# Layer 2's first product in seven block products instead of eight, with streamed weights and a list schedule for the second half

## The chip, the cores and the metric

The program runs on one core of a Trainium2 chip. The metric is device time in microseconds (us), the median of three runs. The engines are TensorE (PE, matrix products), VectorE (DVE), ScalarE (ACT), GpSimd (POOL) and SyncE (SP, which here issues all DMAs).

## The reference, cut to what matters

Attention with a decaying state gives x, 3072 tokens of 512 features; two feed-forward layers follow.

```python
x = attn_out.transpose(0, 2, 1, 3).reshape(3072, 512)
h = x @ moe_w_in               # layer 1: 512 -> 2048
x = np.maximum(0.01 * h, h) @ moe_w_out      # 2048 -> 512
h = x @ moe2_w_in              # layer 2: 512 -> 2048
g = np.where(h > 0.0, h, np.exp(np.minimum(h, 0.0)) - 1.0)
out = g @ moe2_w_out           # 2048 -> 512
```

The weights come as 64-bit floats, and the kernel turns them into 32-bit ones by operations on their bits.

## The kernel before

Tokens are cut into six blocks of 512 (`j`, `NB` = 6), the 2048 inner features into sixteen tiles of 128 (`m`, `MF` = 16), the 512 features into four chunks. Every matrix operand is held as a high and a low part (`hi`, `lo`, type fp32r), and each product of two such operands is three matmuls: high by high, high by low, low by high. A step is one pair of block and tile: `gemm1` makes the tile h of 128 by 512 in one PSUM bank with 12 matmuls (four chunks by three), an activation follows, `split_g` makes its two parts (`ghi` on ACT, `glo` on DVE), and `gemm2` adds the tile's share to the four banks `y` of the block with 12 matmuls. `ph` is 0 in layer 1 and 1 in layer 2.

The order of the work is that of the code, engine by engine; the program adds waits where data or a buffer demands them. Three stretches matter. From about 69 to 153 us the first steps of layer 1 are emitted by `scheduled`: tasks with an engine, a cost and dependencies are placed by a greedy rule, always the task that can begin first, the more urgent one among equals. From about 175 to 525 us steps of layer 1 alternate with attention for later blocks, and `pre` converts layer 2's weights: 32 pieces of 128 by 512, each loaded, converted on ACT and DVE, split on ACT and POOL, and written to DRAM (`wscr`). After that come the last block of layer 1 (block 5, from `NA` on) and layer 2, about 620 to 1142 us. There all weights of layer 2 lie in SBUF, loaded once by `load_w2` into the places of layer 1's, and each step runs `gemm1` for tile s, the activation (`elu_act`, four ACT instructions; `elu_dve`, four DVE instructions one step later), and `gemm2` for tile s-3:

```python
nta = elu_act(h)
if last is not None:
    split(s - 1, last, nc.vector)
d = drain(s - 3, stage_o)
last = elu_dve(h, *nta)
```

`drain` calls `gemm2`, and behind a block's last tile copies the four banks out and stores them: `yscr` in DRAM for layer 1, `out` for layer 2. Layer 2 loads a block of `yscr` back (`load_x`) and splits it into `xhi` and `xlo` (`split_x`).

Of the kernel before, what the change touches and what calls it, by code (L numbers as in the profile page):

```python
# [32 lines left out]
P = 128  # L33
# [11 lines left out]
V0 = 4  # L45

# [8 lines left out]
def body(ctx: ExitStack, tc: tile.TileContext, kkv, w1, w2, tabs, out):  # L55
# [10 lines left out]
    wscr = [dp.tile([P, 4, BLK], F32, name=f"wscr{m}") for m in range(MF)]  # L66
# [9 lines left out]
    nload = nload2 = 0  # L76
# [20 lines left out]

    def load_w2():

        nonlocal nload2  # L100
        m = nload2
        for a in range(2) if m < V0 else (0,):
            n = 1 if m < V0 else 2
            t = place(m, a, n, F32R, "w")
            nc.sync.dma_start(out=t.bitcast(F32), in_=wscr[m][:, 2 * a : 2 * (a + n), :].rearrange("p a c -> p (a c)"))
            for i in range(n):
                wt[1, m, a + i] = t[:, i * W : (i + 1) * W]
        nload2 += 1

# [111 lines left out]
    through = []  # L221

    def pre_load():
        k = npre
        if k < 2 * MF:
            t = cv.tile([P, W], U32, tag="f", name="raw2")
            m, a = divmod(k, 2)
            nc.sync.dma_start(out=t, in_=w2[m][:, a * BLK : (a + 1) * BLK].bitcast(U32))
            through.append(t)
# [3 lines left out]
    def pre(more):  # L233
# [5 lines left out]
        m, a = divmod(npre, 2)  # L239
        npre += 1  # L240
        if more:
            pre_load()
        both = cv.tile([P, W], U16, tag="e", name="e2")
        e, sg = both[:, :BLK], both[:, BLK:]
        f = cv.tile([P, BLK], F32, tag="s", name="f2", bufs=1)
# [3 lines left out]
        top(t, f)  # L249
        low(t, f)  # L250
        sign(e, sg)
        power(e, f)
        r = t.bitcast(F32R)
        nc.scalar.copy(r[:, :BLK], f)
        nc.gpsimd.tensor_tensor(r[:, BLK:], f, r[:, :BLK].bitcast(F32), ALU.subtract)
        nc.sync.dma_start(out=wscr[m][:, 2 * a : 2 * a + 2, :], in_=r.rearrange("p (a c) -> p a c", a=2).bitcast(F32))
# [97 lines left out]
    with ExitStack() as actx:  # L354
# [330 lines left out]
        for n, (s, upto) in enumerate(plan[NL:], NL):  # L685
# [17 lines left out]
            if vi > 3:  # L703

                if m == 2 and npre < 2 * MF:
                    pre_load()
                if 2 < m < MF - 1:
                    pre(m < MF - 2)
# [4 lines left out]
    with ExitStack() as ectx:  # L713
        ep = ectx.enter_context(tc.tile_pool(name="ep", bufs=2))
        eps = ectx.enter_context(tc.tile_pool(name="eps", bufs=3, space=PSUM))
        xs = {}

        def stage_o():
            for _ in range(4):
                yield ep.tile([P, BLK], F32, tag="osb", name="osb", bufs=4)  # L720

        def load_x(j, i):
            t = ep.tile([P, 2, BLK], F32, tag="xs", name="xs")
            nc.sync.dma_start(out=t, in_=yscr[j][:, 2 * i : 2 * i + 2, :])
            xs[j, i] = t

        def split_x(j, k):
            b, t = j % 2, xs[j, k // 2][:, k % 2, :]
            nc.scalar.copy(xhi[b][:, k, :], t)
            nc.vector.tensor_tensor(xlo[b][:, k, :], t, xhi[b][:, k, :].bitcast(F32), ALU.subtract)  # L730

        def elu_act(h):
            n = ep.tile([P, BLK], F32, tag="n", name="n")
            t = ep.tile([P, BLK], F32, tag="t", name="t")
            a = ep.tile([P, BLK], F32, tag="a", name="a2")
            nc.scalar.activation(n, h, AF.Relu, scale=-1.0)  # L736
            nc.scalar.activation(t, n, AF.Tanh, scale=-0.5)  # L737
            nc.scalar.activation(a, t, AF.Copy, bias=-0.5, scale=0.5)
            nc.scalar.activation(n, n, AF.Exp, scale=-1.0)  # L739
            return n, t, a  # L740

        def elu_dve(h, n, t, a):
            gf = gp.tile([P, BLK], F32, tag="gf", name="gf2", bufs=2)
            nc.vector.scalar_tensor_tensor(out=a, in0=n, scalar=1.0, in1=a, op0=ALU.add, op1=ALU.mult)  # L744
            nc.vector.scalar_tensor_tensor(out=t, in0=n, scalar=1.0, in1=t, op0=ALU.add, op1=ALU.mult)  # L745
            nc.vector.scalar_tensor_tensor(out=t, in0=a, scalar=2.0, in1=t, op0=ALU.add, op1=ALU.mult)  # L746
            nc.vector.scalar_tensor_tensor(out=gf, in0=h, scalar=0.0, in1=t, op0=ALU.max, op1=ALU.add)  # L747
            return gf

        def split(s, gf, eng):  # L750
            if s % 4 == 3:
                split_g(s, gf, eng, ep, 1)
            else:
                split_g(s, gf, eng, gp, 3)

        comes = {(0, len(VISITS[0]) - 1): 0, **{(1, j): j + 1 for j in range(NB - 1)}}
        last = None
        for s in range(NA, 2 * NS):
            ph, j, m, (_, _, m0, m1, vi) = steps[s]
            if s % 4 == 0:  # L760
                h = ps.tile([P, BLK], F32, tag="h", name="h")
            else:
                h = eps.tile([P, BLK], F32, tag="h2", name="h2")
            gemm1(ph, m, j % 2, h)
            if ph == 0:
                gf = leaky(h)
                d = drain(s - (2 if s < NA + 4 else 3), stage_o)
                split(s, gf, nc.vector)
            else:
                nta = elu_act(h)  # L770
# [76 lines left out]
```

## Time and profile before

| | before |
|---|---|
| median of three runs | 1148.68 us (1148.34 to 1148.70) |
| profiled execution, first to last instruction (span) | 1146.8 us |
| PE busy | 1132.1 us, 99% of the span |
| DVE busy | 650.8 us, 57% |
| ACT busy | 542.7 us, 47% |
| bytes moved by DMA | 117.10 MB |

No time of its own is given for the profiled execution beside its span; the median of the runs is 1.9 us more than the span, which is what lies around the first and the last instruction. Busy time counts an engine's own instructions and not its waits. PE's instructions overlap, so a busy PE need not be one at its peak; what tells is the time from one matmul to the next. In the rows, L268 is `gemm1`, L291 `gemm2`, L562 the second product in `scheduled`, L736 to L747 the activation of layer 2, L274 and L275 the split of g, L325 the copies out of PSUM.

### The profile page before, as it was taken

Reading aid. Unit: us, or ns where it says so; the run is one execution under the profiler, and the core shown is the slowest. Engines: PE = TensorE matmul, PEld = TensorE weight load, DVE = VectorE, ACT = ScalarE, POOL = GpSimd, SP = SyncE. Lnnn points to the kernel's source line nnn. Section 1 sums busy time; section 2 is a strip of 40 time slices with the busy share of each in tenths; the row PEclk is TensorE's granted clock in tenths of the full one; section 3 lists DMA queues with packets and bytes.
Section 4 is the critical chain, followed back from the end, with each engine's and each line's share of the span. In section 5 each row is a group of like instructions: output and inputs, shape, how many; then the busy total and the mean of one; then the engine's idle time right before and its main releaser. Section 6 shows DMA issues by size and latency. Waiting matters only on the chain.

```text
span 1146.8 us, 14900 instructions
## 1 busy us (share of the span) xinstructions
PE 1132.1 (99%) x6024; PEld 928.2 (81%) x6024; DVE 650.8 (57%) x1047; ACT 542.7 (47%) x899; POOL 92.7 (8%) x77
## 2 busy tenths in 40 slices
PE   8899999999999999999999999999999999999998
PEld 6678888788888888888888888888888888888886
DVE  5999913246544663641213766765765666666655
ACT  2576621234444443432324655555555655655553
POOL 4000001102222221210000000000000000000000
PEclk9999999999999999999999999999999999999999
DMA  9912313345544544522556200100100100000100
GB/s 377 418 41 89 131 37 111 111 135 201 200 161 167 190 178 139 193 93 68 189 185 219 92 19 1 55 19 1 55 19 1 55 19 1 37 1 1 38 1 37
DMA packets 29302, 117.10 MB, mean 102 GB/s; under 512 B 3249, under 2 KB 3249, under 8 KB 23217
## 3 DMA queue, kind: packets, MB, share of 16 engines
q1 hardware_dynamic: 29232, 116.15, 27.4%
q8 instruction: 47, 0.77, 0.3%
q14 instruction: 23, 0.18, 0.1%
HBM read 84.68 MB, written 31.46 MB: 101 GB/s over the span
## 4 chain that ended last, share of the span: by engine, by line
PE 94%; DVE 4%; DMA 1%; ACT 0%; issue 0%; SPq 0%; ACTq 0%
PE h L268 44%; PE y L291 41%; PE y L562 4%; PE sc L398 2%; PE o L416 2%; DMA kv<-in_kkv 1%; PE o L424 1%; PE o L420 1%; DVE f L127 1%; DVE pt L404 0%; DVE f L134 0%; DVE xlo L441 0%; DVE e L131 0%; DVE w L181 0%; DVE s L116 0%; DVE f L123 0%
## 5 line engine op out<-in xcount | busy, mean ns | idle before, releaser
L268 PE MATMUL h<-xhi,w 128*128 128x512 f32 x1536 | 505.7, 391 | 1.1 <-ACT gf L350 1.1
L268 PEld LDWEIGHTS h<-xhi,w 128*128 128x128 f32 x1536 | 288.2, 188 | 63.1 <-ACT gf L350 1.5
L275 DVE TENSOR_TENSOR glo<-gf,ghi 128x512 fp32r<-128x512 f32 x171 | 119.3, 698 | 370.5 <-ACT ghi L274 370.5
L268 PE MATMUL h<-xlo,w 128*128 128x512 f32 x768 | 299.0, 389 | 0.0
L291 PE MATMUL y<-w,ghi 128*128 128x512 f32 x768 | 236.4, 389 | 0.0
L291 PE MATMUL y<-ghi,w 128*128 128x512 f32 x616 | 204.3, 393 | 0.0
L291 PEld LDWEIGHTS y<-w,ghi 128*128 128x128 f32 x768 | 144.1, 188 | 29.9
L268 PEld LDWEIGHTS h<-xlo,w 128*128 128x128 f32 x768 | 144.2, 188 | 29.5
L736 ACT ACTIVATE n<-h 128x512 f32<-128x512 f32 x96 | 57.5, 599 | 224.3 <-PE h L268 224.3
L291 PE MATMUL y<-w,glo 128*128 128x512 f32 x384 | 149.4, 389 | 0.0
L350 ACT ACTIVATE gf<-h 128x512 f32<-128x512 f32 x96 | 57.2, 596 | 186.7 <-PE h L268 186.3
L291 PEld LDWEIGHTS y<-ghi,w 128*128 128x128 f32 x616 | 115.6, 188 | 26.4 <-issue 2.4
L291 PE MATMUL y<-glo,w 128*128 128x512 f32 x308 | 119.9, 389 | 0.0
L274 ACT CAST ghi<-gf 128x512 fp32r<-128x512 f32 x171 | 104.7, 612 | 5.3 <-DVE gf L747 3.4
L291 PEld LDWEIGHTS y<-w,glo 128*128 128x128 f32 x384 | 72.2, 188 | 15.0
L744 DVE SCALAR_TENSOR_TENSOR a<-n,a 128x512 f32<-128x512 f32 x96 | 65.7, 685 | 5.9 <-ACT n L739 5.9
L746 DVE SCALAR_TENSOR_TENSOR t<-a,t 128x512 f32<-128x512 f32 x96 | 66.4, 692 | 3.3
L747 DVE SCALAR_TENSOR_TENSOR gf<-h,t 128x512 f32<-128x512 f32 x96 | 66.4, 691 | 3.3
L291 PEld LDWEIGHTS y<-glo,w 128*128 128x128 f32 x308 | 57.8, 188 | 11.6
L120 ACT ACTIVATE e<-e,ebias 128x512 int16<-128x512 uint16 (+1 forms) x52 | 42.7, 821 | 50.7 <-DVE e L117 50.5
L745 DVE SCALAR_TENSOR_TENSOR t<-n,t 128x512 f32<-128x512 f32 x96 | 65.9, 686 | 0.0
L737 ACT ACTIVATE t<-n 128x512 f32<-128x512 f32 x96 | 60.7, 632 | 3.1
(59 smaller groups left out, 924.8 us busy)
## 6 DMA issues: line engine op xcount, KB each, us to landing
kv<-in_kkv SPq DMA_DIRECT2D x23, 1024.0 KB, 6.5
raw<-in_w SPq DMA_DIRECT2D x40, 512.0 KB, 3.8
wscr<-raw SPq DMA_DIRECT2D x32, 512.0 KB, 2.6
raw<-in_w SPq DMA_DIRECT2D x12, 1024.0 KB, 12.3
w<-wscr SPq DMA_DIRECT2D x12, 1024.0 KB, 4.8
xs<-yscr SPq DMA_DIRECT2D x12, 512.0 KB, 3.6
out<-osb SPq DMA_DIRECT2D x24, 256.0 KB, 3.8
yscr<-ysb SPq DMA_DIRECT2D x16, 256.0 KB, 2.7
```

The lines of the kernel that those rows point to most:

```text
L268: nc.tensor.matmul(h, a, x, start=(n == 0), stop=(n == 3 * KD - 1))
L274: nc.scalar.copy(ghi, gf)
L275: eng.tensor_tensor(glo, gf, ghi.bitcast(F32), ALU.subtract)
L291: nc.tensor.matmul(acc[d], lhsT, rhs, start=(first and n == 0), stop=(last and n == 2))
L350: nc.scalar.activation(gf, h, AF.Prelu, alpha=0.01)
L562: nc.tensor.matmul(acc[i][:, d % 2], lhsT, rhs, start=(m == m0 and n == 0), stop=(m == m1 - 1 and n == 2))
L736: nc.scalar.activation(n, h, AF.Relu, scale=-1.0)
L737: nc.scalar.activation(t, n, AF.Tanh, scale=-0.5)
L744: nc.vector.scalar_tensor_tensor(out=a, in0=n, scalar=1.0, in1=a, op0=ALU.add, op1=ALU.mult)
L745: nc.vector.scalar_tensor_tensor(out=t, in0=n, scalar=1.0, in1=t, op0=ALU.add, op1=ALU.mult)
L746: nc.vector.scalar_tensor_tensor(out=t, in0=a, scalar=2.0, in1=t, op0=ALU.add, op1=ALU.mult)
L747: nc.vector.scalar_tensor_tensor(out=gf, in0=h, scalar=0.0, in1=t, op0=ALU.max, op1=ALU.add)
```

## The change

Layer 2's first product is done for two token blocks at once (`q` = 0, 1, 2 stands for blocks 2q and 2q+1) and for two tiles at once (`i` and `i + 8`), so that one group is a product of 2 by 2 blocks: X11, X12, X21, X22 (token block by half of the 512 features) times W11, W12, W21, W22 (half of the features by tile). Strassen's scheme in Winograd's form needs seven products of 6 matmuls where the plain way has eight:

```
S1 = X21+X22   S2 = S1-X11   S3 = X11-X21   S4 = X12-S2
T1 = W12-W11   T2 = W22-T1   T3 = W22-W12   T4 = T2-W21
bank px:  X11 W11 | + S2 T2 -> copied for h12 | + S3 T3 -> h22 | - X22 T4 -> h21
h11 = X11 W11 (copied from px) + X12 W21 (bank pv)
h22 += S1 T1 (bank pq);   h12 += S1 T1 + S4 W22 (bank pq, added to)
```

(h11 and h12 are the two tiles of block 2q, h21 and h22 those of block 2q+1.) The T's are made once, in `pre`, in the stretch of attention: eight of the 32 conversions get five more instructions on DVE, two on ACT and one on POOL, and with their eight neighbours they write seven operands per group to `w1scr`. The S's are made on DVE once for each pair of blocks: four instructions of 1024 elements a partition, and the split of seven X operands is seven such instructions on ACT and seven on DVE.

From the second step of block 5 on, everything is tasks of one list: PE's order is fixed (two or three pieces of second products behind each product, a piece being the three matmuls of one bank), ACT, DVE and SP are ordered by the greedy rule. The h tiles are copied from PSUM to SBUF and have the activation in place there; up to 32 of them and their successors live in the places that layer 1's weights leave. The second products run through the blocks in order; the first of layer 2 stands behind five groups, so behind ten tiles of block 0. Weights are no longer kept: each product loads its operand of 256 KB (`w1r`, six buffers), each second product's tile its 512 KB (four buffers), again for each block: 264 loads in place of 20.

```diff
-    def load_w2():
...
-            nc.sync.dma_start(out=t.bitcast(F32), in_=wscr[m][:, 2 * a : 2 * (a + n), :].rearrange("p a c -> p (a c)"))
...
+        i, n = m - HM, QB
+        fi = kept.pop(i)
...
+        sub(tw[:, 1, 1], g[:, n:], g[:, :n], ALU.subtract)
+        sub(tw[:, 0, 1], g[:, :n], gi[:, :n], ALU.subtract)
+        sub(g[:, :n], g[:, n:], tw[:, 0, 1], ALU.subtract)
+        sub(gi[:, n:], gi[:, n:], g[:, :n], ALU.subtract)
+        nc.scalar.copy(tt[:, :, 0], tw[:, :, 1])
+        sub(tt[:, :, 1], tw[:, :, 1], tw[:, :, 0], ALU.subtract)
+        nc.sync.dma_start(out=w1scr[i][:, 3:5, :], in_=t.bitcast(F32).rearrange("p (b c) -> p b c", b=2))
+        halves_of(g, pw)
+        nc.scalar.copy(fi[:, :n], gi[:, n:])
+        nc.gpsimd.tensor_tensor(fi[:, n:], gi[:, n:], gi[:, :n], ALU.subtract)
...
+        stock["w1"] = [lazy(lambda k=k: ep.tile([P, BLK], F32R, name=f"w1r{k}")) for k in range(6)]
+        stock["g"] = [lazy(lambda k=k: ep.tile([P, BLK], F32, name=f"g{k}")) for k in range(4)]
...
+        ORDER = ("11", "12", "s2", "s1", "s3", "22", "s4")
+        PAUSE = (2, 2, 2, 2, 3, 2, 3)
...
+            task(("mk", q, "s1"), "V", 1.25, [("ld", q, "21"), ("ld", q, "22")],
+                 lambda rt=rt: mix(rt("s"), rt("21"), rt("22"), add), use=[T("21"), T("22")], take=("t", T("s")))
...
+                    task(("xh", q, n), "A", 1.05, [seen, ("mk", q, n) if n != "22" else ("ld", q, "22")],
+                         lambda q=q, n=n, src=src: x_hi(q, n, src), use=[key], take=("x", X(n)))
...
+        def product(q, i, k):
+            n = ORDER[k]
+            hi, lo = at(("x", q, n))
+            w = at(("w1", q, i, k))
+            to = bank[("px", "pv", "px", "pq", "px", "px", "pq")[k]]
+            first = k in (0, 1, 3)
+            z = 0
+            for c in range(2):
+                wh, wl = w[:, c * P : (c + 1) * P], w[:, QB + c * P : QB + (c + 1) * P]
+                for a, x in ((wh, hi[:, c]), (wh, lo[:, c]), (wl, hi[:, c])):
+                    nc.tensor.matmul(to, a, x, start=(first and z == 0), stop=(z == 5), skip_group_check=True)
+                    z += 1
...
+            def snap(b, k):
+                task(("c", *hk[b]), "A", 0.62, [P_(k)], lambda: nc.scalar.copy(at(("h", *hk[b])), bank["px"]), take=("g", ("h", *hk[b])))
+
+            def plus(b, name, deps):
+                t = ("h", *hk[b])
+                task(("s", *hk[b]), "V", 0.7, [("c", *hk[b])] + deps, lambda: tt(at(t), at(t), bank[name], add), use=[t])
...
+            return [prod(0, [prior("c", "21")]), prod(1, [prior("s", "11")]), prod(2, [("c", *hk["11"])]),
+                    prod(3, [prior("s", "12"), freed]), prod(4, [("c", *hk["12"])]), prod(5, [("c", *hk["22"])]), prod(6, [("s", *hk["22"])])]
...
+        filler(48)
+        before = None
+        for q in range(SB):
+            for i in range(HM):
+                for x, n in zip(group_tasks(q, i, before), PAUSE if q < SB - 1 or i < HM - 2 else (1, 2, 2, 1, 2, 2, 2)):
+                    put_pe(x)
+                    filler(n)
+                before = q, i
+        filler(10**6)
```

The seven products are numbered k = 0 to 6 in the order of `ORDER`; p0 to p6 below. A product waits for the copy or the addition that frees its bank: the last lines of `group_tasks` name them.

On PE, before, in layer 2 (h2 is the bank of a first product, y the banks of a second one, numbers tell buffers apart), a second product and the next first one stand like this:

```order
L291 MATMUL y1_7187<-w_4907,ghi_7520 128x512 x2
L291 MATMUL y1_7187<-w_4907,glo_7521 128x512
L268 MATMUL h2_7623<-xhi1_100,w_5055 128x512
L268 MATMUL h2_7623<-xlo1_102,w_5055 128x512
L268 MATMUL h2_7623<-xhi1_100,w_5055 128x512 x2
```

On PE, now, in the third group of the second pair of blocks: p4, three pieces of second products (of 3 matmuls each), p5, the next piece. Here xhi0 and xlo0 are places that now hold both parts of one X operand, ws a streamed weight of the second product:

```order
L996 MATMUL px_4535<-xhi0_107,w1r2_4615 128x512 x6
L1083 MATMUL y_4585<-ws_5407,ghi_4663 128x512 x2
L1083 MATMUL y_4585<-ws_5407,glo_4668 128x512
L1083 MATMUL y_4585<-ws_5407,ghi_4663 128x512 x2
L1083 MATMUL y_4585<-ws_5407,glo_4668 128x512
L1083 MATMUL y_4586<-ws_5407,ghi_4663 128x512 x2
L1083 MATMUL y_4586<-ws_5407,glo_4668 128x512
L996 MATMUL px_4535<-xlo0_109,w1r3_4635 128x512 x6
L1083 MATMUL y_4586<-ws_5407,ghi_4663 128x512 x2
```

The 12 matmuls of a first product in a row have become products of 6 between pieces of second products, and p5 adds to the bank px that p4 wrote, behind 9 matmuls.

On ACT, before, in layer 2, a step is the four activation instructions and the cast of the tile before:

```order
L736 ACTIVATE n_7077<-h2_7064 128x512
L737 ACTIVATE t_7078<-n_7077 128x512
L738 ACTIVATE a2_7079<-t_7078 128x512
L739 ACTIVATE n_7077<-n_7077 128x512
L274 CAST ghi_7084<-gf2_7059 128x512
```

On ACT, now, around the copy of px that lies between that p4 and p5 (the first `L1014` row; nt and a2 are the activation's scratch):

```order
L1095 CAST ghi_4620<-ws_5372 128x512
L1046 ACTIVATE nt_4823<-nt_4823 128x512
L1014 COPY g0_4802<-px_4535 128x512
L1050 ACTIVATE a2_4824<-nt_4823 128x512
L1054 ACTIVATE nt_4823<-nt_4823 128x512
L1042 ACTIVATE nt_4883<-ws_5523 128x512
L1046 ACTIVATE nt_4883<-nt_4883 128x512
L1014 COPY g1_4838<-px_4535 128x512
```

The copies stand between the activation instructions of other tiles, whose scratch (two sets) DVE gives back.

On DVE, now, the addition that p6 of the same group waits for is the `L1018` row; ahead of it stand the activation of an earlier tile and a split:

```order
L1066 SCALAR_TENSOR_TENSOR nt_4883<-a2_4884,nt_4883 128x512
L1098 TENSOR_TENSOR glo_4627<-ws_5372,ghi_4620 128x512
L1070 SCALAR_TENSOR_TENSOR ws_5677<-ws_5677,nt_4883 128x512
L1018 TENSOR_TENSOR g0_4802<-g0_4802,pq_4537 128x512
L1058 SCALAR_TENSOR_TENSOR a2_4824<-nt_4823,a2_4824 128x512
```

The addition is new. Before, a bank of a first product was read by ACT's L736 and, last, by DVE's L747, with four banks in turn; now px is read by copies on ACT alone, and pv and pq by additions on DVE.

## Rows read from the trace of the kernel before

**Rows 1.** The page: span, and its first part (busy time, share, instructions).
```profile
span 1146.8 us, 14900 instructions
...
PE 1132.1 (99%) x6024; PEld 928.2 (81%) x6024; DVE 650.8 (57%) x1047; ACT 542.7 (47%) x899; POOL 92.7 (8%) x77
```

**Rows 2.** Windows: stretch, its length, busy time (instructions) by engine, clock, DMA share, GB/s.
```profile
69.00:153.00 84.00, 83.72 (x369) 69.36 (x370) 73.32 (x95) 52.92 (x63) 1.28 (x1) 1.00 0.26 101
175.00:525.00 350.00, 350.00 (x2196) 284.08 (x2195) 167.18 (x312) 134.00 (x224) 72.61 (x56) 1.00 0.43 154
...
620.00:1142.00 522.00, 522.00 (x2305) 432.17 (x2303) 332.45 (x510) 291.74 (x508) 0.00 (x0) 1.00 0.08 28
```

**Rows 3.** The page: the chain that ended last, by engine.
```profile
PE 94%; DVE 4%; DMA 1%; ACT 0%; issue 0%; SPq 0%; ACTq 0%
```

**Rows 4.** The chain by time, last 28 us: start, length, what.
```profile
1123.26 2.72 PE h L268 x12
...
1131.42 10.89 PE y L291 x48
...
1142.34 0.58 ACT osb L325
```

**Rows 5.** Groups with shapes apart, 620 to 1142 us: ACT.
```profile
L737 ACT ACTIVATE t<-n 128x512 f32<-128x512 f32 x95 | 60.1, 632 | 3.0
...
L274 ACT CAST ghi<-gf 128x512 fp32r<-128x512 f32 x96 | 58.1, 605 | 3.4 <-DVE gf L747 3.4
L736 ACT ACTIVATE n<-h 128x512 f32<-128x512 f32 x95 | 56.9, 599 | 220.1 <-PE h L268 220.1
...
L325 ACT COPY osb<-y 128x512 f32<-128x512 f32 x12 | 6.4, 581 | 0.0
```

**Rows 6.** The same view and stretch: DVE.
```profile
L275 DVE TENSOR_TENSOR glo<-gf,ghi 128x512 fp32r<-128x512 f32 x96 | 66.5, 692 | 181.3 <-ACT ghi L274 181.3
L746 DVE SCALAR_TENSOR_TENSOR t<-a,t 128x512 f32<-128x512 f32 x95 | 65.7, 692 | 3.3
```

**Rows 7.** The same view, whole span: 1024 elements wide.
```profile
L181 DVE TENSOR_TENSOR w<-f,w 128x1024 fp32r<-128x1024 f32 x12 | 14.6, 1220 | 0.6 <-ACT w L177 0.6
...
L177 ACT CAST w<-f 128x1024 fp32r<-128x1024 f32 x12 | 12.6, 1051 | 9.1 <-DVE f L134 9.1
```

**Rows 8.** Timeline, 800 to 812 us: start, length, instruction, [idle before it].
```profile
801.97 0.60 ACT L274 CAST ghi<-gf 128x512 fp32r<-128x512 f32 x1
...
802.61 0.69 DVE L275 TENSOR_TENSOR glo<-gf,ghi 128x512 fp32r<-128x512 f32 x1 [2.09 <-ACT ghi L274]
...
804.63 0.39 PE L268 MATMUL h<-xhi,w 128*128 128x512 f32 x1
...
805.06 0.60 ACT L736 ACTIVATE n<-h 128x512 f32<-128x512 f32 x1 [1.52 <-PE h L268]
```

**Rows 9.** DMA issues: KB each, median us from issue to landing.
```profile
xs<-yscr SPq DMA_DIRECT2D x12, 512.0 KB, 3.6
out<-osb SPq DMA_DIRECT2D x24, 256.0 KB, 3.8
yscr<-ysb SPq DMA_DIRECT2D x16, 256.0 KB, 2.7
```

**Rows 10.** The same timeline: four stores issued by SP.
```profile
803.93 1.94 SPq L326 DMA_DIRECT2D out<-osb  x4
```

**Rows 11.** The page: GB/s moved in each of the 40 slices.
```profile
GB/s 377 418 41 89 131 37 111 111 135 201 200 161 167 190 178 139 193 93 68 189 185 219 92 19 1 55 19 1 55 19 1 55 19 1 37 1 1 38 1 37
```

**Rows 12.** Waits of PE, 69 to 153 us: us in total, times, longest.
```profile
PE y L562 <- DVE glo L593: 0.6, 1, 0.6
```

**Rows 13.** Timeline, 346 to 356 us: a step that converts a weight piece.
```profile
351.10 0.66 ACT L113 COPY e<-raw 128x512 int16<-128x512 int16 x1
...
354.66 0.62 ACT L254 CAST raw<-f 128x512 fp32r<-128x512 f32 x1 [1.44 <-DVE f L134]
...
355.39 0.60 ACT L350 ACTIVATE gf<-h 128x512 f32<-128x512 f32 x1
```

More of the change, by code (lines that the diff above doesn't have):

```diff
@@ L231, in body, with halves_of, pre @@
     npre = 0
-    def pre(more):
+    def halves_of(f, r):
+        nc.scalar.copy(r[:, 0], f)
+        nc.gpsimd.tensor_tensor(r[:, 1], f, r[:, 0].bitcast(F32), ALU.subtract)
+    def pre(more, pool):
         nonlocal npre
@@ L713, in body @@
     with ExitStack() as ectx:
[L714 to L725, printed above, removed]
@@ L784, in body @@
-        split(2 * NS - 1, last, nc.vector)
-        drain(2 * NS - 1, stage_o)
+        ep = ectx.enter_context(tc.tile_pool(name="ep", bufs=1))
+        eps = ectx.enter_context(tc.tile_pool(name="eps", bufs=1, space=PSUM))
+        bank = {n: eps.tile([P, BLK], F32, tag=n, name=n) for n in ("px", "pv", "pq")}
+        bank["h"] = ps.tile([P, BLK], F32, tag="h", name="h")
+        drain(NA - 2, stage_f)
+        gemm1(0, 0, (NB - 1) % 2, bank["h"])
+        drain(NA - 1, stage_f)
+        ys = [ps.tile([P, 2, BLK], F32, tag=f"y{i}", name="y") for i in range(2)]
@@ new lines, in body, with task @@
+        ybank = [ys[d // 2][:, d % 2] for d in range(4)]
+        J = NB - 1
+        tasks, uses, uses_of, places, pe = {}, {}, {}, {}, []
+        def task(key, eng, cost, deps, fn, use=(), take=None, lag=0.0):
+            tasks[key] = eng, cost, [d for d in deps if d is not None], fn, take, lag
+            uses_of[key] = list(use) + ([take[1]] if take else [])
+            for u in uses_of[key]:
+                uses.setdefault(u, []).append(key)
+            if eng == "P":
+                pe.append(key)
@@ new lines, in body, with at, lazy, get @@
+        stock = {}
+        turns_into = {}
+        made = {}
+        def at(key):
+            return places[key]()
+        def lazy(make):
+            got = []
+            def get():
+                if not got:
+                    got.append(make())
+                return got[0]
+            return get
+        def part(get, *index):
+            return lambda: get()[index]
+        def slot(m, dtype=F32R):
+            return lazy(lambda: wp.tile([P, 4, BLK], dtype, tag=f"w{m}", name="ws"))
@@ new lines, in old_second, with old_leaky @@
+        def old_second(s, d):
+            m = steps[s][2]
+            w = wt[0, m, 1]
+            ds = slice(d * P, (d + 1) * P)
+            hi, lo = w[:, ds], w[:, BLK + d * P : BLK + (d + 1) * P]
+            ghi, glo = at(("ghi", s)), at(("glo", s))
+            for n, (a, x) in enumerate(((hi, ghi), (hi, glo), (lo, ghi))):
+                nc.tensor.matmul(ybank[d], a, x, start=(m == 0 and n == 0), stop=(m == MF - 1 and n == 2))
+        def old_leaky(s):
+            nc.scalar.activation(at(("gf", s)), bank[old_bank(s)], AF.Prelu, alpha=0.01)
@@ new lines, in body, with old_steps @@
+        last_of = {}
+        def old_steps():
+            before = None
+            for s in range(NA, NS):
+                m = s - NA
+                for k in range(KD):
+                    yield ("g1", s, k), 0.68 if m else 0.0, [("leaky", s - (2 if m < 5 else 1))] if k == 0 and m > 1 else [], \
+                        (lambda s=s, k=k: old_first(s, k) if s > NA else None), [("w", m), ("x5",)]
+                if before is not None:
+                    yield from old_seconds(before)
+                before = s
+            yield from old_seconds(before)
@@ L788, in _tables @@
+        assert len(over) == len(tasks), [x for x in tasks if x not in over][:20]
 def _tables():
```

385 lines of the change are left out of this document (312 added, 73 removed).

## The prediction

> **What bounds the kernel now.** I read the page first: PE is busy for 1132.1 of the 1146.8 us [rows 1], and the chain of work that ended last is 94% PE [rows 3]. Then the windows, because a share of busy time is a mean over stages: in layer 2, 620 to 1142 us, PE is busy in all 522.00 us at a granted clock of 1.00, while DVE works 332.45 us of them (64%) and ACT 291.74 (56%) [rows 2]. The reader is to see that nothing but the number and the pace of the matmuls sets the end there. The pace is in the chain by time: 12 matmuls take 2.72 us in either product [rows 4], 0.2267 us each. So a matmul left out is worth 0.2267 us for as long as PE still never waits, and the whole question is whether it will.
>
> **What is removed.** Layer 2's first product has 6 blocks by 16 tiles by 12 = 1152 matmuls. Now there are 24 groups of 7 products of 6 = 1008. The 144 matmuls that are gone are all of the same shape as those that stay (512 columns), and at 0.2267 us they are 32.6 us. No matmul is added anywhere: the sums T and S are made on other engines, and adding into px and pq is the accumulation that PSUM does for any product. The second products keep their 1152.
>
> **What is added, per group.** A group makes four tiles and takes along 16 pieces of second products, four tiles' worth: 42 + 48 = 90 matmuls, 20.4 us of PE. In that time:
> DVE runs 16 activation instructions and 4 splits at 0.692 us [rows 6], 13.84 us, and 3 additions. No such addition (SBUF plus PSUM) is in this trace; L275, the same size, takes 0.692, and I use that: 2.08 us. The S's and the splits of X are 11 instructions for 8 groups, at 1.22 us [rows 7] 1.7 us per group. Sum 17.6 us, 86% of 20.4.
> ACT runs 16 activation instructions at no more than 0.632, 4 casts at 0.605, 4 copies of px (L736 reads PSUM at the same size in 0.599) and per group one copy out of y at 0.581 [rows 5]; 7 wide casts at 1.051 for 8 groups [rows 7] add 0.9. Sum 16.4 us, 80%.
> So both stay below PE, but DVE with 2.8 us to spare per group in place of 36%. There is a precedent in the same trace: in the stretch from 69 to 153 us, which the same kind of list orders, DVE is busy 73.32 of 84 us (87%), and PE 83.72 [rows 2]; its only wait there is 0.6 us, once [rows 12]. This is the row on which I lean most.
>
> **The waits on the way.** Which product can be held up is read from the order. p5 is the tightest: it adds to px behind three pieces, 2.04 us, in which ACT must copy px. A copy takes 0.60; the hand from PE to ACT takes 0.04 us (the matmul at 804.63 ends at 805.02, ACT starts at 805.06), and from ACT to DVE as much (802.57, 802.61) [rows 8]. If a wide cast of 1.05 has just begun, the copy still ends 0.04 + 1.05 + 0.60 = 1.69 us after p4, plus a hand back of some 0.04. It fits. p6 has 4.76 us for that copy and one addition of 0.69; the other products have 4.08 us or more. The h tiles have a lead: the shortest is that of the last tile of an even block, made by p6 of a pair's last group and used 15 pieces of 0.68 and six products of 1.36 later, 18 us, for a chain of one addition, four ACT and four DVE instructions, a cast and a split, 7.3 us. Each wait costs nothing while these covers last; uncovered, PE waits for what is missing.
>
> **The loads.** A group needs 7 x 256 KB and 4 x 512 KB, 3.9 MB in 20.4 us, 193 GB/s. Layer 2 moves 28 GB/s now [rows 2], but the second slice of the span shows 418 [rows 11], and from 175 to 525 us PE is busy in every one of the 350 us beside 154 GB/s [rows 2]. A load of 512 KB lands after 3.6 us, one of 256 KB I bound by 2.7 and 3.8 [rows 9]; the six buffers of w1r give each about 17 us, the four of w2 15 us, and 8 us in the last stretch, where only second products are left (three tiles of 2.72). SP issues four stores in 1.94 us [rows 10], 0.49 each, so 13 or so in a group cost it 6.3 us. All of it is hidden; a load that came later than these leads would stop its product and, SP being one queue, the loads behind it.
> The Trainium skill (DMA: Bandwidth & Descriptors, Rules for kernel authors) asks for 1 MiB or more per DMA for the most bandwidth, which speaks against cutting 1 MB weights into 256 KB pieces. The rows differ in what matters here: four stores of 256 KB leave within 1.94 us and land 3.8 us after their issue, so they overlap [rows 9, 10]. The sum above uses the rows and comes to 1117; by the rule, taken so far that each small load pays for itself one after the other, it is rival (c), 1427.
>
> **The stretch of attention.** Eight conversions get five more DVE instructions (at most 0.69 each), two ACT, one POOL. PE has no work in them. In a step that converts, ACT's cast ends at 355.28 and the next leaky starts at 355.39 [rows 13], so what is added moves that leaky back, by 1.2 us (two short copies) to 4.7 (the five DVE instructions in full as well). The next product in the same bank comes three pieces of 2.72 us later, 8.2 us. DVE is busy 167.18 and ACT 134.00 of 350 us there [rows 2]. Cost nothing; if the cover failed, at most 4.7 us eight times, which I hold for very unlikely. The loads of kv are issued two chunks ahead and only move behind a few more stores on SP.
>
> **The beginning and the end.** ACT's order puts two casts of the first X blocks ahead of the leaky of block 5's third step, and their loads now stand on SP behind block 4's four stores (1.94 us). Such a step has 5.44 us for 1.9 us of leaky, cast and split, so a lateness of 2 to 3 us is about used up: 0 to 4 us, I take 1.5. Behind the last matmul (1131.42 + 10.89 = 1142.31) ACT's two copies of 0.58 go out one after the other; now ACT and DVE share them: 0.4 us less, 0 to 0.6.
>
> **The sum.** 1146.8 - 32.6 + 1.5 - 0.4 = 1115.3 us of span. The median of the runs lies 1.9 us above the span: **1117 us**, 2.8% less.
>
> **The rivals.**
> (a) ACT is late for px. Two instructions ahead of the copy in place of one make 0.04 + 1.05 + 0.63 + 0.60 + 0.04 = 2.36 against 2.04 us: 0.3 us for each of 24 groups, 8 us, 1125. For it: the copy stands among the activations of other tiles, and those wait for scratch that DVE gives back. Against it: the greedy rule prefers the more urgent task, and hands take 0.04 us where the list's costs count 0.2.
> (b) DVE is the bound in part. Its additions wait for PE's products, and while one waits all that is queued behind it on DVE stands still. If each of the three loses w, a group takes 17.6 + 3w; above w = 0.93 us PE is held up. At 1.1 us: 20.9, 0.5 us by 24 groups = 12 us, 1129. The Trainium skill (TensorE: Matmul & The Clock Gate, Architectural detail, on the engines' queues) has VectorE's queue as strict first in, first out; the trace agrees as far as L275 goes, which stood idle for 181.3 us in 96 times, 1.9 us each, waiting for ACT [rows 6].
> (b') The same, to the other side: from w = 1.4 us on (21.8 us per group) the 32.6 us are used up, and at the 1.9 us just shown it is 23.3, 2.9 by 24 = 70 us, 1187: slower than before. Against it: those 1.9 us are idle time of an engine that had nothing else to do, and the stretch from 69 to 153 us shows 87% without it.
> (c) The loads don't overlap. One after the other a group needs 7 x 2.7 + 4 x 3.6 = 33.3 us [rows 9], 12.9 more than 20.4, over 24 groups 310 us: 1427. It decides from 21.8 us per group on. The four overlapping stores speak against it.
> (d) The saving is eaten before layer 2, by the eight conversions: 8 x 4.7 = 38 us if nothing covered them, 1155. The 8.2 us speak against it.
>
> **How the numbers follow.** The forecast (PE still never waits for more than a few us): 0.62, by itself 1114 to 1121. (a) 0.12, 1121 to 1128. (b) 0.16, 1121 to 1146. (b') 0.05. (c) 0.02. (d) 0.01. Something else that PE doesn't see: 0.02, no change. A measurement of this kernel tells about 0.2%, 2.3 us, from no change. Faster: 0.62 + 0.12 + 0.16 and a little of the rest, 0.91; within 0.2%: 0.02; slower: 0.07. The range from 1113.5 to 1128 holds nearly all of the forecast, (a), and the lower third of (b): eight in ten. Its lower end is the sum with no wait at the beginning and 0.6 us at the end (1146.8 - 32.6 - 0.6 + 1.9 = 1115.5) and 2 us for what I may have missed.
>
> **What would show it.** Right: 144 fewer matmuls at an unchanged 2.72 us for twelve; PE without idle time from 70 us to the end; DVE busy some 86% and ACT 80% while groups run; 190 GB/s or so in layer 2. (a) would show as PE waiting for the copies of px, (b) as waits for DVE's additions or for the splits, with DVE idle ahead of its additions; (c) as PE waiting for w1r or ws from DMA; (d) as waits between 175 and 525 us. The prediction is wrong if PE's idle time grows by over 10 us, wherever that is.

## The result, and the profile after

The changed kernel takes 1117.92 us (median of four runs, 1116.78 to 1120.26) against 1148.69 us (median of four runs of the kernel before), a ratio of 0.973 with an interval from 0.972 to 0.975. The profiled execution took 1116.78 us with a span of 1115.0 us, 31.8 us less than the span in [rows 1].

The page of the changed kernel, its answer to [rows 1, 3] and, in the last two rows, to [rows 9]:

```profile
span 1115.0 us, 15688 instructions
...
PE 1100.6 (99%) x5880; PEld 901.1 (81%) x5880; DVE 731.8 (66%) x1156; ACT 618.3 (55%) x1020; POOL 100.6 (9%) x85
...
PE 93%; DVE 4%; ACT 1%; DMA 1%; issue 0%; ACTq 0%
...
ws<-w2scr SPq DMA_DIRECT2D x96, 512.0 KB, 4.0
w1r<-w1scr SPq DMA_DIRECT2D x168, 256.0 KB, 3.1
```

There are 144 fewer matmuls, and PE is busy 31.5 us less. The other engines work more than before, DVE by 81 us and ACT by 76, and yet PE's share of the span is what it was, and that of the chain is 93% in place of 94%. So the added work must lie beside PE. The windows say where:

```profile
69.00:153.00 84.00, 83.66 (x369) 69.28 (x370) 73.36 (x95) 53.03 (x63) 1.35 (x1) 1.00 0.26 101
175.00:525.00 350.00, 350.00 (x2197) 284.05 (x2195) 190.12 (x352) 140.15 (x240) 79.79 (x64) 1.00 0.49 172
...
640.00:680.00 40.00, 39.85 (x176) 32.69 (x175) 24.95 (x38) 29.66 (x52) 0.00 (x0) 1.00 0.73 232
680.00:800.00 120.00, 120.00 (x531) 99.35 (x530) 109.64 (x158) 91.23 (x155) 0.00 (x0) 1.00 0.71 221
800.00:1080.00 280.00, 280.00 (x1237) 231.63 (x1236) 203.51 (x312) 195.06 (x338) 0.00 (x0) 1.00 0.66 203
620.00:1110.00 490.00, 489.85 (x2161) 405.10 (x2160) 357.62 (x536) 336.07 (x576) 0.00 (x0) 1.00 0.65 202
```

Against [rows 2] the stretch of attention has 23 us more of DVE, 6 of ACT and 7 of POOL, and PE is full in it as before. In layer 2 PE is full from 680 to 1080 us at a granted clock of 1.00. The reader is to see the stretch from 680 to 800 us: DVE is busy 91% of it, and PE loses nothing. The chain by time then gives the pace of a group; its rows in layer 2 repeat every 20.40 us, 90 matmuls of 0.2267:

```profile
844.07 2.04 PE y L1083 x9
...
864.47 2.04 PE y L1083 x9
...
884.87 2.04 PE y L1083 x9
...
905.27 2.04 PE y L1083 x9
...
1049.43 61.32 PE y L1083 x270
```

From 1049.43 us on the chain names nothing but matmuls, 270 in 61.32 us. What the copies and additions cost, and how long ACT and DVE stood idle ahead of them, is in the groups with shapes apart, 620 to 1110 us. Here `ws` is a place in SBUF that holds an h tile; the copies and additions into the other places (`g`) have rows of their own and cost the same:

```profile
L1098 DVE TENSOR_TENSOR glo<-ws,ghi 128x512 fp32r<-128x512 f32 x83 | 57.2, 689 | 63.8 <-ACT ghi L1095 63.2
...
L1014 ACT COPY ws<-px 128x512 f32<-128x512 f32 x76 | 44.7, 588 | 49.8 <-PE px L996 49.1
L1018 DVE TENSOR_TENSOR ws<-ws,pq 128x512 f32<-128x512 f32 x39 | 26.8, 687 | 27.1 <-PE pq L996 24.3 <-ACT ws L1014 2.5
L1018 DVE TENSOR_TENSOR ws<-ws,pv 128x512 f32<-128x512 f32 x19 | 13.1, 687 | 7.7 <-PE pv L996 4.6 <-ACT nt L1054 2.7
```

ACT stood still for 49.8 us ahead of these 76 copies of px, so as a rule it was there before the product was done. Read one by one in the timeline, 86 of all 96 copies begin 0.04 us after the product's last matmul, nine more within 0.35 us, and one, at 664.65 us, 1.23 us after it. DVE stood idle for 27.1 + 7.7 us ahead of these 58 additions, 0.6 us each.

PE's own waits, whole span, in order of size (the first and the last of eight groups, 9.6 us in all):

```profile
PE o L454 <- DVE pt L442: 4.4, 4, 1.6
...
PE sc L436 <- DVE e L122: 0.2, 1, 0.2
```

None of the eight is a wait of the list that orders layer 2. Two shorter ones are not among them; the timeline shows one, at 666.29 us (start, length, instruction, idle time before it):

```profile
663.70 1.05 ACT L932 CAST xhi<-xhi 128x1024 fp32r<-128x1024 f32 x1 [1.35 <-DMA xhi<-yscr]
...
664.65 0.58 ACT L1014 COPY ws<-px 128x512 f32<-128x512 f32 x1
...
665.65 0.59 ACT L875 COPY ws<-y 128x512 f32<-128x512 f32 x1
...
666.29 0.50 PE L865 MATMUL y<-ghi,w 128*128 128x512 f32 x1
```

A wide cast waits 1.35 us for its load, the copies behind it on ACT come later, and the bank of y comes free at 665.65 + 0.59 = 666.24. At the pace of the rows around it this matmul would have started at 665.98, so 0.3 us are lost, and 0.1 more until the next one. The other wait is at 538.90 us, of the same size, where ACT's two copies of block 4's banks (1.07 us) stand ahead of a leaky.

### The profile page after: what moved, and what is told of

The parts are those of the page before. It is cut to its first block, busy times and chain, and to the rows that moved or that the text cites. A ratio compares the mean times of both kernels' runs of the same rounds, so it can differ in the third digit from the quotient of the medians.

```text
span 1115.0 us, 15688 instructions
## 1 busy us (share of the span) xinstructions
PE 1100.6 (99%) x5880; PEld 901.1 (81%) x5880; DVE 731.8 (66%) x1156; ACT 618.3 (55%) x1020; POOL 100.6 (9%) x85
## 4 chain that ended last, share of the span: by engine, by line
PE 93%; DVE 4%; ACT 1%; DMA 1%; issue 0%; ACTq 0%
PE y L1083 23%; PE h L306 18%; PE y L329 15%; PE px L996 11%; PE pq L996 6%; PE y L600 4%; PE y L865 4%; PE h L856 3%; PE pv L996 3%; PE sc L436 2%; PE o L454 2%; PE o L462 1%; PE o L458 1%; DVE pt L442 1%; DVE f L118 1%; DVE f L125 0%
## 5 line engine op out<-in xcount | busy, mean ns | idle before, releaser
L1083 PE MATMUL y<-ws,ghi 128*128 128x512 f32 x768 | 236.4, 389 | 0.0
L306 PE MATMUL h<-xhi,w 128*128 128x512 f32 x648 | 214.3, 392 | 1.1 <-ACT gf L388 1.1
L1083 PEld LDWEIGHTS y<-ws,ghi 128*128 128x128 f32 x768 | 144.0, 188 | 30.2 <-ACT ws L875 0.2
L1083 PE MATMUL y<-ws,glo 128*128 128x512 f32 x384 | 149.4, 389 | 0.0
L306 PEld LDWEIGHTS h<-xhi,w 128*128 128x128 f32 x648 | 121.6, 188 | 28.5 <-ACT gf L388 1.5
L306 PE MATMUL h<-xlo,w 128*128 128x512 f32 x324 | 126.2, 390 | 0.0
L313 DVE TENSOR_TENSOR glo<-gf,ghi 128x512 fp32r<-128x512 f32 x59 | 45.0, 763 | 115.1 <-ACT ghi L312 113.2
L1014 ACT COPY ws<-px 128x512 f32<-128x512 f32 x83 | 48.8, 588 | 55.3 <-PE px L996 54.0
L996 PE MATMUL px<-ws,w1r 128*128 128x512 f32 x288 | 73.1, 389 | 0.0
L996 PE MATMUL pq<-ws,w1r 128*128 128x512 f32 x288 | 73.1, 389 | 0.0
L306 PEld LDWEIGHTS h<-xlo,w 128*128 128x128 f32 x324 | 60.8, 188 | 12.2
```

What stands on the lines that cost most here:

```text
L306: nc.tensor.matmul(h, a, x, start=(n == 0), stop=(n == 3 * KD - 1))
L313: eng.tensor_tensor(glo, gf, ghi.bitcast(F32), ALU.subtract)
L996: nc.tensor.matmul(to, a, x, start=(first and z == 0), stop=(z == 5), skip_group_check=True)
L1014: task(("c", *hk[b]), "A", 0.62, [P_(k)], lambda: nc.scalar.copy(at(("h", *hk[b])), bank["px"]), take=("g", ("h", *hk[b])))
L1083: nc.tensor.matmul(ybank[d], a, x, start=(first and n == 0), stop=(last and n == 2))
```

## The experiments

Each kernel below is the changed one with one edit; two of the last ones have a second edit, which is named there. Ratios are to the kernel before.

**Eight products in place of seven.** p1 is computed twice, all else stands where it stood.

```diff
+            for _ in range(2 if k == 1 else 1):
```

> The changed kernel, but the second product of each group (X12 by W21, into bank pv) is done twice, the second time over the first, so the 144 matmuls that the scheme leaves out are back on PE and all else stays in the order it had. Theory (PE is the bound, everything added is hidden): the changed kernel's 1117.9 us plus 24 x 1.36 = 32.6, so 1150.5 us, within 0.4% of the kernel before; PE's pace and its waits as in the changed kernel. Rival (DVE, ACT or the loads share the bound): they get 1.36 us more room per group, so less than the 32.6 us comes back, 1125 to 1145 us. Rival (the list and the streaming gain something of their own): below 1148 us.

Measured: 1149.89 us, ratio 1.0006 [0.9996, 1.0015]. The window from 700 to 1100 us:

```profile
700.00:1100.00 400.00, 400.00 (x1766) 331.05 (x1765) 299.30 (x451) 275.30 (x474) 0.00 (x0) 1.00 0.62 193
```

With the matmuls back, all that the scheme adds (the S and T, the copies, the additions, the streamed weights, the list) costs 1.2 us, taken together, against the kernel before. And the 144 matmuls are worth 1149.89 - 1117.92 = 32.0 us. So the gain comes from the matmuls that were left out; the rest of the change gives and takes about a microsecond in sum. DVE and ACT have 1.36 us more per group here than in the changed kernel, but PE is full in these stretches of both, so they hold nothing up in either.

**How much room DVE has.** One more DVE instruction (the maximum of a tile with itself, which changes nothing) for each h tile, 2.8 us per group; then two. The list is not told of them.

```diff
                 nc.vector.scalar_tensor_tensor(out=x, in0=x, scalar=0.0, in1=t, op0=ALU.max, op1=ALU.add)
+                for _ in range(1):        # second kernel: range(2)
+                    tt(x, x, x, ALU.max)
```

> The changed kernel with one more DVE instruction of 128x512 per h tile behind the last one of the activation (the larger of x and x, so nothing changes), 0.69 us, 2.8 us per group; the list doesn't know of it. In the changed kernel DVE was busy 81% from 680 to 1040 us and 91% from 680 to 800. Theory (DVE has room to spare, 2.8 us per group by my count): all or nearly all hidden, 1118 to 1130 us, waits where X operands are made. Rival (DVE's additions hold its queue, so that DVE is close to the bound as it stands): the full 24 x 2.8 = 66 us show, about 1184.

> As the run before with two more DVE instructions per h tile, 5.5 us per group. Theory: 81% and 27% are over the whole, so PE now waits for DVE: some 1.5 to 2.8 us per group in 19 to 24 groups, 30 to 67 us, 1148 to 1185. Rival (DVE is the bound as it stands): 24 x 5.5 = 132 us, about 1250. If DVE's instructions overlap so much that its true load is far below its busy time: below 1130.

Measured: 1133.02 us (0.986 [0.984, 0.988]) and 1191.01 us (1.036 [1.034, 1.038]). The window of most of layer 2 with one instruction:

```profile
680.00:1040.00 360.00, 351.61 (x1531) 287.20 (x1530) 320.61 (x486) 251.58 (x440) 0.00 (x0) 1.00 0.66 204
```

The same window with two:

```profile
680.00:1040.00 360.00, 325.86 (x1372) 261.23 (x1371) 331.15 (x498) 225.97 (x393) 0.00 (x0) 0.97 0.59 184
```

And PE's two longest waits with two:

```profile
PE pq L996 <- DVE ws L1018: 22.5, 12, 3.8
PE px L996 <- ACT ws L1014: 11.2, 8, 2.1
```

With one instruction more, the longest wait and the longest for an addition (500 us to the end) are these; L875 is the copy of a bank y behind a block's last tile:

```profile
PE y L1085 <- ACT ws L875: 2.4, 2, 1.8
...
PE pq L996 <- DVE ws L1018: 1.7, 2, 1.0
```

DVE is busy 89% and 92%. With two instructions more PE waits above all for DVE's additions, with the copies late as well; with one its waits are short and lie at several places, and none of them is for an X operand, where I had expected them. Both times came out above what I expected (by 3 and by 6 us at the upper end), and below the rivals. DVE as a bound, as in rival (b), is real, it only lies further out: with 2.8 us more per group the kernel loses 15 us, with 5.5 us more it loses 73 us and is slower than before. The step from one to two costs four times the first. Part of that is the clock: from 680 to 1040 us the granted clock is 0.97 with the waits. PE's busy time over the span grows by 23.8 us (1100.6 to 1124.4) for the same 5880 matmuls, but not all of that is the clock, for in the run with one piece of cover (below) it grows by 6.2 us (to 1106.8) at a granted clock of 1.00.

**How much room ACT has.** Two ACT copies of the scratch onto itself for each h tile, 4.9 us per group, first unknown to the list (the diff), then as two tasks of their own between the last ACT and the first DVE instruction of the activation, each with a planned cost of 0.61 us.

```diff
                 nc.scalar.activation(n, n, AF.Exp, scale=-1.0)
+                for _ in range(2):
+                    nc.scalar.copy(n, n)
```

> The changed kernel with two more ACT instructions of 128x512 per h tile (the last activation result copied onto itself), 0.6 us each, 4.9 us per group; the list doesn't know of it. ACT was busy 74% from 680 to 1040 us, so 98% now. Theory (ACT has 4 us per group to spare by my count): mostly hidden, 1118 to 1140 us, with waits of PE for the copies of px. Rival (the copies of px are at their limit as it stands): each further instruction ahead of a copy adds 0.6 us to it, four copies in a group, 24 groups: 58 us, about 1176.

> As the run with two more ACT instructions per h tile, but each is a task of the list with its cost, so that the copies of px keep their place in time. That run came out at 1161 us, 43 more than the changed kernel, with 19 waits of PE of 1.1 us for copies of px. Theory (ACT has the room for 4.9 us per group on the whole, and what was lost came from copies that stood behind instructions the list did not know): most of the 43 us come back, 1118 to 1135 us. Rival (ACT's load itself, 98% of the time with its wide casts, is the bound): 1150 us or more, as before.

Measured: 1161.21 us (1.011 [1.009, 1.012]) unknown, 1120.16 us (0.974 [0.973, 0.976]) known. The window of the first:

```profile
680.00:1040.00 360.00, 340.21 (x1442) 272.61 (x1441) 261.87 (x390) 313.29 (x544) 0.00 (x0) 0.98 0.63 195
```

Its longest wait of PE, in total, times, longest one:

```profile
PE px L996 <- ACT ws L1014: 21.4, 19, 2.7
```

The window of the second:

```profile
680.00:1040.00 360.00, 360.00 (x1590) 298.27 (x1589) 272.26 (x403) 318.22 (x555) 0.00 (x0) 1.00 0.68 212
```

For the first I had expected 1140 at most, by a sum of busy times: that theory fell. The second kernel has the same instructions, with ACT busy 88% of the stretch, and PE is full; its 2.2 us over the changed kernel lie within the spread of both. So it is not ACT's capacity that runs out in the first, it is its order: the copy of px stands behind instructions that the list did not count, and the product waits for it 19 times. Read one by one, 17 of its 96 copies begin within 0.06 us of the product's end, and the latest 4.3 us after it; in the second kernel 94 of 96 begin within 0.17 us. This is rival (a), and its price when the order is wrong is 43 us, not 8. One thing is not separated: in the first kernel the two copies hang on the instruction before them, so that nothing can come between, in the second they are tasks of their own; how much of the 43 us is the wrong cost and how much the longer piece, no run shows.

**The cover of p5 alone.** One piece of second products between p4 and p5 in place of three; the other two go behind p6.

```diff
-        PAUSE = (2, 2, 2, 2, 3, 2, 3)
+        PAUSE = (2, 2, 2, 2, 1, 2, 5)
```

> The changed kernel with one piece (0.68 us) of second products between p4 and p5 in place of three, and five behind p6 in place of three; the list is made anew with that. The copy of px between p4 and p5 needs 0.04 + 0.60 + 0.04 = 0.68 us even with nothing ahead of it on ACT. Theory (that copy is what the three pieces cover): PE waits there, from nothing up to the 1.05 us of one ACT instruction in its way, 0.3 to 0.7 us per group, 7 to 17 us, 1125 to 1135, and the waits stand at px for ACT. Rival (ACT's place in the list always leaves it free at that moment, the pieces cover nothing): 1117 to 1120.

Measured: 1124.70 us (0.979 [0.977, 0.980]), 6.8 us more than the changed kernel and a shade below the 1125 expected. The edit reaches 22 of the 24 groups (the last two have pauses of their own, as the diff of the change shows), so that is 0.31 us for each, at the lower end of the 0.3 to 0.7 expected. The wait shows on the weight load of p5, which goes ahead of its matmul (640 to 1040 us):

```profile
PEld px L996 <- ACT ws L1014: 8.3, 18, 0.9
```

The cover is 0.68 us here where the hand-overs and the copy take 0.04 + 0.60 + 0.04. With three pieces it is 2.04, and no weight load or matmul of px waits for a copy in the changed kernel's trace. In that kernel's last two groups only two pieces stand there, 1.36 us, and that is enough too.

**Two buffers for w1r in place of six.**

```diff
-        stock["w1"] = [lazy(lambda k=k: ep.tile([P, BLK], F32R, name=f"w1r{k}")) for k in range(6)]
+        stock["w1"] = [lazy(lambda k=k: ep.tile([P, BLK], F32R, name=f"w1r{k}")) for k in range(2)]
```

> The changed kernel with two buffers for the operands of the products in place of six. A buffer is free when its product ends, and the product after next begins 4.08 us later or a little more; in the changed kernel's trace such a load lands 3.1 us after its issue. Theory (loads overlap each other and other work, and the lead of six buffers is far more than is needed): 0 to 0.5 us per product where a load of 512 KB stands ahead of it on SP, 168 products, 0 to 40 us, 1118 to 1158, the waits at the products for w1r. Rival (loads pay one after the other, and the six buffers are what hides it): 300 us more, over 1400.

Measured: 1127.31 us (0.981 [0.979, 0.982]). From 560 us on PE waits 4.5 us in the profiled execution; these two are put down to loads, the other 1.5 us to ACT:

```profile
PE px L996 <- DMA w1r<-w1scr: 2.0, 4, 0.8
PE pq L996 <- DMA w1r<-w1scr: 1.0, 3, 0.5
```

A load can now start only when the product two before is done, 4.08 us ahead of its own (two pauses and a product of 1.36 each), and still comes almost in time, for 256 KB land in 2.9 us (median of 168): the price is 9.4 us in all, 0.4 per group. Rival (c), 1427 us, falls with this and with the 202 GB/s of the changed kernel.

**The beginning of the list.** Three runs look at the first of the two places where the changed kernel's list makes PE wait. In the first, block 4's four copies all go to DVE, so that ACT's leaky of block 5 comes sooner:

```diff
-                (nc.vector.tensor_copy if d < 2 else nc.scalar.copy)(t, acc[d])
+                (nc.vector.tensor_copy if d < 2 or j == NB - 2 else nc.scalar.copy)(t, acc[d])
```

> The changed kernel, but all four copies out of PSUM behind block 4 go to DVE, so that ACT can take the leaky of block 5's first step 1 us sooner. In the changed kernel that step's second product waited there for its low part, 0.3 us and 0.1 for starting again. Theory: that wait is gone from the trace, 0.4 us, which the times can't tell: 1116.5 to 1120. Rival (DVE's two further copies make the split as late as the leaky was): the wait stays, or grows to 0.7 us.

Measured: 1118.35 us (1117.17 to 1120.81; 0.973 [0.971, 0.975]), no difference in time. The wait at 538.90 us is gone, and in the profiled execution, whose span is 1119.0 us, another has come:

```profile
539.60 0.43 SPq L920 DMA_DIRECT2D xlo<-yscr  x1
...
549.51 1.04 ACT L932 CAST xlo<-xlo 128x1024 fp32r<-128x1024 f32 x1 [3.69 <-DMA xlo<-yscr]
...
550.46 0.59 ACT L868 ACTIVATE gf<-h 128x512 f32<-128x512 f32 x1
...
551.76 0.79 PE L865 MATMUL y<-ghi,w 128*128 128x512 f32 x1 [2.29 <-ACT ghi L907]
```

A load of 512 KB, issued at 539.60, let its cast begin at 549.51; the list had counted on 2.2 us behind an issue that it puts at 1.7. The leaky of block 5's third step stands behind that cast on ACT and comes late, and PE stands for 2.29 us. That is the lateness which the prediction's part on the beginning describes. In the changed kernel's own profile the same load landed sooner, 7.3 us after its issue, and PE did not wait there:

```profile
xlo<-yscr SPq DMA_DIRECT2D x1, 512.0 KB, 7.3
```

In the next two kernels the list is told a longer landing time for these four loads, 12 us and then 5, on top of the edit above:

```diff
-                task(("ld", q, b), "Q", 1.7, written + [prev], ..., lag=2.2)
+                task(("ld", q, b), "Q", 1.7, written + [prev], ..., lag=2.2 if q else 12.0)
```

> The first four loads of layer 2 are planned to land 12 us after their issue in place of 2.2, and block 4's four copies out of PSUM all go to DVE. If the lateness at the start of the list (a load that takes near 10 us, ACT's casts of the first X blocks ahead of block 5's activations) is what makes some runs 2 to 3 us longer, the wait of the second products near 539 us and the one behind the late cast are both gone, and the time is 1116 to 1117.5 us with a spread below that of the changed kernel (1116.8 to 1120.3). Rival: the spread has nothing to do with these loads; then the median lies at 1117 to 1119 with the same spread.

> As the run with a planned landing time of 12 us for the first four loads of layer 2, but with 5 us. ACT's second cast of an X block now stands behind the third activation of block 5 and not ahead of it, and the rest of the order is as in the changed kernel. If a planned time that is too long is what moved the first S and their splits behind the product that needs them, and one that is too short is what makes the second products wait near 550 us, this one has neither wait: 1115.5 to 1117 us, every run below 1118, with PE full from 540 to 640 us. Rival: casts ordered for a later landing push DVE's chain of S and splits back here too, and PE waits some microseconds for the first split: 1119 to 1126.

Measured: 1127.80 us (0.981 [0.980, 0.983]) with 12, 1122.12 us (0.976 [0.975, 0.978]) with 5. The changed kernel itself, once more beside the first of them:

> The changed kernel itself once more, on the same chip, for the spread: 1116.5 to 1120.5 us, median near 1118, with a start of the list that waits 0.5 to 3 us near 539 us.

Measured: 1117.43 us (1116.95 to 1117.97; 0.973 [0.972, 0.974]), a spread of 1.0 us where the first set of runs had 3.5. Its wait near 539 us is 0.3 us and 0.1 for starting again, a little less than expected; at the other place, where a bank of y comes free (667.40 us there), it waits 1.0 us. In the kernel with 12 us, the timeline has the first product of layer 2 like this:

```profile
575.74 2.50 PE L996 MATMUL px<-xhi,w1r 128*128 128x512 f32 x5 [7.88 <-DVE xhi L936]
```

And these are the windows around it:

```profile
565.00:570.00 5.00, 2.86 (x13) 2.04 (x11) 1.05 (x2) 1.21 (x2) 0.00 (x0) 1.00 0.00 0
570.00:575.00 5.00, 0.00 (x0) 0.00 (x0) 4.90 (x5) 1.58 (x2) 0.00 (x0) 0.57 0.00 0
575.00:580.00 5.00, 4.26 (x10) 3.40 (x11) 4.93 (x5) 3.93 (x5) 0.00 (x0) 0.50 0.13 25
580.00:585.00 5.00, 5.00 (x21) 4.05 (x21) 3.35 (x4) 0.00 (x0) 0.00 (x0) 0.90 0.26 82
```

With 5 us the same wait is 2.5 us, the longest of PE from 500 us on:

```profile
PE px L996 <- DVE xhi L936: 2.5, 1, 2.5
```

In both kernels PE waits for no leaky any more, and both are slower, by 9.9 and 4.2 us: the idea that a longer planned landing time would bring the time down to 1116 or 1117 fell, and the rival of the run with 5 us was right. Their spreads, 2.8 and 2.2 us, are no smaller than that of the changed kernel's second set. Told that the loads come late, the list puts DVE's S and splits behind them late too, and now the first product of layer 2 waits for a split. In the changed kernel that split (558.06 to 559.28 us) is done 6.7 us ahead of its product at 566.02. Of the three planned times tried, the 2.2 us of the changed kernel is the best, though the loads take longer; values below it were not tried.

## Why the prediction was right

The time came out as forecast (1117 us), and the mechanism is the forecast one: PE stays full, and the matmuls left out are the gain. That it came out to the microsecond is partly luck, for runs of the changed kernel lie 3.5 us apart, and the 1.5 us for the beginning was a choice between 0 and 4. The steps one by one:

**What is removed.** 144 matmuls at an unchanged pace of 20.40 us for 90. The span fell by 31.8 us; the run with eight products puts the worth of the matmuls at 32.0. The term was 32.6.

**DVE and ACT per group.** From 680 to 1040 us DVE is busy 290.52 and ACT 266.27 of 360 us, 81% and 74%, where the prediction had 86% and 80%. Each instruction costs what its row of before gave: the addition, which no row had shown, 0.687 us (0.692 taken), the copy of px 0.588 (0.60). The percentages are means again: most of the S's and the splits of X for the second and third pair of blocks fall on 680 to 800 us, 91%, and but for three splits (875 to 882 us) they are missing later. The precedent of 87% from 69 to 153 us was a good guide, and 91% is now another.

**The waits on the way.** p5 is the tightest, as the order showed, and 2.04 us cover it; the run with one piece gives the price when they don't. The prediction took that cover for all 24 groups. In the last two it is 1.36 us, and that of the other copies goes down from 4.08 to 3.40; PE waits in neither. The rival (a) would have needed ACT to be late; on the mean it was early by 0.7 us per copy (49.8 us in 76). The rival (b) needed more than 0.93 us lost on each addition; DVE stood idle 0.6 ahead of one. The runs with more DVE instructions add load and no lost time, so they test the bound and not the cause that (b) gives for it: with 2.8 us more the time is in the range of (b), with 5.5 us more the kernel is slower than before, as in (b').

**The loads.** 202 GB/s in layer 2 (193 estimated), 256 KB landing in 3.1 us and 512 KB in 4.0, and no wait of PE for one. The 1 MiB rule of the Trainium skill (DMA: Bandwidth & Descriptors, Rules for kernel authors) does not decide here: one after the other, the loads of a group would take 7 x 3.1 + 4 x 4.0 = 37.7 us, and PE goes through a group in 20.40, so pieces of a quarter and a half of that size overlap, and the kernel needs no more than they move.

**The stretch of attention.** Its last step comes 0.07 us later than before (a second product starts at 508.39 us, at 508.32 before), and the 0.07 us are there ahead of it (a first product starts at 151.01 us, at 150.94 before), so the eight dearer conversions cost nothing and rival (d) falls.

**The beginning and the end.** The beginning was put at 0 to 4 us, 1.5 taken. In the profile it is 0.4 us, and another 0.4 comes at 666.29 us, where a second product waits for a bank of y; the prediction has no term for that bank. In the profiled execution of the kernel with block 4's copies on DVE the beginning took 2.3 us and the slower restart. There the wait is the forecast one, a leaky behind a late cast; in the changed kernel's own profile that wait did not come, and its 0.4 us are ACT's copies of block 4 ahead of a leaky. The prediction had 512 KB landing after 3.6 us; here the second of these loads took 7.3. The end gave 0.25 us where 0.4 was taken (4.25 us from the last matmul to the end of the span, 4.5 before). So -32.6 + 0.1 + 0.8 - 0.25 = -32.0 against the measured -31.8; the 0.2 us that are left I can't place.

**What I had too low.** The prediction's price for (a), 8 us, has one copy per group late by 0.3 us. When ACT's order was wrong, 79 of 96 copies were late by up to 4.3 us and the price was 43 us, with ACT busy 87%; no sum of busy times shows that. For DVE the sum is the better guide: with two more instructions it gives 17.6 + 5.5 = 23.1 us per group, over 24 groups 65 us more than 20.4, and 73 were measured; with one more it gives 20.4, so nothing, and 15 were measured.

## What to carry to other kernels

A kernel that is 99% one engine gains what is taken off that engine, if the work that replaces it fits beside it: count the added instructions per group by rows of the same size, then look in the order for the shortest cover between a result and the instruction that needs its place, and widen that one. What a list of planned costs leaves free is not the share of idle time: ACT busy 88% held nothing up when the list knew of its work, and at 87% it cost 43 us when it didn't, so keep the planned costs true and test the room both ways. A planned time that is too long is not safe either: with 12 and 5 us in place of 2.2 for four loads the list put other work too late, and the kernel lost 9.9 and 4.2 us.

## What the hardware showed that I had not expected

A wait of PE costs more than its length. In the kernel with the 12 us landing time (its row and windows are above) PE did nothing from 567.86 to 575.74 us; the granted clock was 1.00 before, 0.57 from 570 to 575 us and 0.50 from 575 to 580, the lower of the two levels (1.2 GHz), and the matmuls there followed each other every 0.426 us (six in 2.56, 578.04 to 580.60) in place of 0.2267. The next six took 1.56 us, so the pace was coming back, and from 582.16 on it is 0.2267 again. The 17 matmuls from 575.74 to 582.16 us took 6.42 us where 3.85 was due, some 2.6 us on top of the 7.9.

A load's landing time varies: 512 KB of a weight land in 4.0 us in the median of 96 in layer 2, and at the start of the list, behind block 4's four stores and some loads, 512 KB of X took 7.3 us in the changed kernel's profile, 8.0 when it was profiled again and 9.9 in the kernel with block 4's copies on DVE. What makes them late there was not tested.

Runs also differ by what happens ahead of all that was changed. The first steps of layer 1 after the list of 69 to 153 us start at 151.01 us in the profile of the changed kernel and at 152.91 in that with the 12 us landing time, though the work up to there is the same, and the whole of the stretch that follows is moved by those 1.9 us. The windows from 8 to 12 us show where it begins, first in the changed kernel, then in the one with 12 us:

```profile
8.00:12.00 4.00, 3.37 (x48) 2.55 (x50) 1.72 (x4) 0.58 (x1) 2.00 (x2) 1.00 1.02 431
```

```profile
8.00:12.00 4.00, 4.00 (x36) 3.12 (x38) 0.57 (x2) 0.58 (x1) 2.00 (x2) 0.63 1.01 427
```

The granted clock is 1.00 in the one and 0.63 in the other. Of the 13 profiles, five show a granted clock of 0.57 to 0.63 there, and the same five start those steps at 152.91 to 153.15 us; the other eight, that of the kernel before among them, show 1.00 and start at 150.72 to 151.35. In both kernels of the two windows PE had stood idle for DVE just ahead, 1.33 us in the changed one and 1.53 in the other; why the clock fell in the one and not in the other stays open.
